# Sliding-window attention and soft MoE: the last experts' weights by column halves, with half-width stores ahead of the last load

## The chip, the core and the metric

The kernel runs on one core of a Trainium2 chip. The metric is the device time of one execution in microseconds. The engines are TensorE (PE; PEld its weight loads), VectorE (DVE), ScalarE (ACT), GpSimd (POOL) and SyncE (SP). Here POOL issues all loads, which turn fp32 in HBM into fp16 on the chip, and SP issues all stores.

## The reference

Eight batches of eight heads, 576 positions of 64 elements, go through causal attention with a window of 64. The result, 4608 rows of 512, goes through a soft mixture of eight experts with four slots each.

```python
scores = np.where((rel >= 0) & (rel < 64), q @ k.T / 8, -1e9)
x = (softmax(scores) @ v).transpose(0, 2, 1, 3).reshape(4608, 512)
logits = x @ phi                       # 4608 x 32 slots
slot_input = softmax(logits, axis=0).T @ x
for e in range(8):                     # 4 slots each
    h = np.maximum(slot_input[e] @ w1[e], 0.0)    # 512 -> 1024
    slot_out[e] = h @ w2[e]                       # 1024 -> 512
out = softmax(logits, axis=1) @ slot_out
```

Each slot's input is a sum over all 4608 rows, so no expert can start before the last row of attention is done, and no row of the result can be formed before the last expert is done.

## The kernel before

**Attention.** A unit is one batch and four of its heads; the sixteen units run one after the other, each in three stages j. `load_unit` issues three loads per unit from POOL. TensorE transposes (`stage_t1`, `stage_t2`), scores (`stage_s`) and weights the values (`stage_av`), ScalarE takes the exponential, VectorE divides and writes the rows x into `xbp`. Once both halves of a batch are there, six steps are spread over the next six stages: `stage_xt` (three transposes of x), `stage_logit` (logits, their exponential ET and column sums esum), `stage_ex` (ET transposed, row sums, their reciprocals crcp) and `stage_slot` (ET times x, added to acc). For the last batch, 7, no unit follows, and the six steps run one behind the other after the loop. Then acc is divided by the sum of esum and written as `slot_oa`, from which four small matmuls (`si`) make the slot inputs `slot_inT`.

**Weights.** `load_w(e, n)` loads a quarter of an expert: n = 0, 1 are halves of w1, n = 2, 3 halves of w2, 512 KB each as landed. They are issued between the units' loads, in the order of `w_order`, expert after expert; what is left at unit 13 is issued at once. A DMA of POOL waits for the eighth before it. w2 of expert 7 (tile `w2l`) has no buffer of its own: it takes one of the two of `xbp` (tag x_bp), after a batch pair is done with it.

**Experts.** `expert_h(e)` multiplies the slot inputs by w1 (16 matmuls of 256 columns, four at a time in different column groups), takes the ReLU on ScalarE, transposes h (`th`) and writes it as `hT`; `expert_o(e)` multiplies by w2 (8 matmuls of 512 columns) and adds into one PSUM tile `sop`. `expert_h(e + 1)` stands ahead of `expert_o(e)`. After expert 7, sop is cast to `slot_oa`, half by ScalarE and half by VectorE.

**The result.** For each of 9 blocks (8 batches, and one of the last 64 rows of all), four matmuls `cp` of 512 columns, each scaled by crcp on ScalarE or VectorE into `ob`, and two stores of 512 KB from SP. The buffers of ob are those of w1 (tag w1s).

**Order.** POOL issues as the code is written. On the other engines a scheduler sets the order, by dependencies and the order of the code.

Of the kernel before, what the change touches and what calls it, by code (L numbers as in the profile page):

```python
# [11 lines left out]
ALU = mybir.AluOpType  # L12
# [4 lines left out]
def kernel(  # L17
# [51 lines left out]
    w1_t, w2_t = {}, {}  # L69

    def load_w(e, n):
# [7 lines left out]
        if n < 2:  # L79
            c = slice(2 * n, 2 * n + 2)  # L80
            nc.gpsimd.dma_start(out=w1_t[e][:, c], in_=moe_w1[e].rearrange("(c p) f -> p c f", p=128)[:, c])  # L81
        else:
            c = slice(4 * n - 8, 4 * n - 4)
            nc.gpsimd.dma_start(out=w2_t[e][:, c], in_=moe_w2[e].rearrange("(c p) d -> p c d", p=128)[:, c])  # L84
# [43 lines left out]
    esum = const.tile([128, B + B // 2], FP32, name="esum")  # L128
# [137 lines left out]

    def stage_logit(b):
# [42 lines left out]

    nu = len(units)
    w_order = [(e, n) for e in range(E) for n in range(4)]
# [33 lines left out]
    stage_av(*pend)  # L346
    while todo:
        todo.pop(0)()
    b = B - 1
    stage_xt(b, 0)  # L350
    stage_xt(b, 1)
    stage_xt(b, 2)
    stage_logit(b)
    stage_ex(b)
    stage_slot(b)
    dinv = const.tile([128, 2], FP32, name="dinv")
    nc.vector.reduce_sum(dinv[:, 0:1], esum[:, :], axis=AXX)
    nc.vector.reciprocal(dinv[:, 1:2], dinv[:, 0:1])
    pa_sb = slot_oa
    nc.scalar.activation(pa_sb[:, 0:256], acc[:, 0:256], AF.Copy, scale=dinv[:, 1:2])  # L360
    nc.vector.tensor_scalar(out=pa_sb[:, 256:512], in0=acc[:, 256:512], scalar1=dinv[:, 1:2], scalar2=None, op0=ALU.mult)
# [4 lines left out]
    for dc in range(NHD):  # L366
        nc.tensor.matmul(si[:, dc, :], pa_sb[:, 128 * dc:128 * dc + 128], sel4[:, :], start=True, stop=True)
# [3 lines left out]
    sop = ps2.tile([128, D], FP32, name="sop", tag="sop", bufs=1)  # L371

    def expert_h(e):
# [6 lines left out]
        h_sb = pet.tile([128, 256], FP16, name="h_sb", tag="h_sb")  # L380
        nc.scalar.activation(h_sb[:, :], hp[:, :], AF.Relu)
        th = ps2.tile([128, 2, 4, SPE], FP32, name="th", tag="th", bufs=1)
        for f in range(2):
            nc.tensor.matmul(th[:, f], h_sb[:, 128 * f:128 * f + 128],
                             sel[:, :, SPE * e:SPE * e + SPE], start=True, stop=True)
# [6 lines left out]
    def expert_o(e):  # L392
        hT = hTs[e % 2]
        for i in range(NFC // 4):
            for g in range(4):
                nc.tensor.matmul(sop[32 * g:32 * g + 32, :], hT[:, 4 * i + g, :], w2_t[e][:, 4 * i + g, :],
                                 start=(e == 0 and i == 0), stop=(e == E - 1 and i == NFC // 4 - 1))

    expert_h(0)
    for e in range(E):  # L400
        if e + 1 < E:
            expert_h(e + 1)
        expert_o(e)
    nc.scalar.copy(out=slot_oa[:, 0:256], in_=sop[:, 0:256])
    nc.vector.tensor_copy(out=slot_oa[:, 256:512], in_=sop[:, 256:512])

    for blk in range(B + 1):
        ob = pw1.tile([128, 4, D], FP32, name="ob", tag="w1s")
        for g in range(4):
            cp = ps2.tile([128, D], FP32, name="cp", tag="cp", bufs=4)  # L410
            nc.tensor.matmul(cp[:, :], ET[:, 4 * blk + g, :], slot_oa[:, :],  # L411
                             start=True, stop=True)
# [5 lines left out]
        if blk < B:  # L418
            for g in range(0, 4, 2):
                nc.sync.dma_start(  # L420
                    out=out[S * blk + 128 * g:S * blk + 128 * g + 256, :].rearrange("(c p) d -> p c d", p=128),
                    in_=ob[:, g:g + 2, :])
        else:
            for o in range(2):
                nc.sync.dma_start(
                    out=out.rearrange("(c o t) d -> o t c d", o=2, t=S)[o, 512:576],
                    in_=ob[64 * o:64 * o + 64, :, :])

# [29 lines left out]
```

## Time and profile before

| | |
|---|---|
| median of 4 runs | 190.06 us (189.43 to 190.56) |
| the profiled execution: time, span | 189.43 us, 187.7 us |
| PE, DVE, ACT, POOL busy | 76%, 58%, 60%, 32% of the span |
| loads: landed by the POOL queue | 30.97 MB |
| stores: by the SP queue | 9.44 MB |
| granted TensorE clock, mean | 0.935 |

The span is from the first to the last instruction; the rest of the time lies around it. The bytes of loads are counted as they land, in fp16, so that 208 GB/s of loads are 416 GB/s read from HBM, while stores are fp32 on both sides. The DMA share is the mean busy share of the 16 DMA engines, and goes over 1 where transfers of one engine overlap. Rows of the profile carry line numbers of the kernel before.

### The profile page before, as it was taken

The page shows a single profiled execution, that of the slowest core. Times are in us where ns is not written, and L with a number is a line of the kernel's source. Part 1 is how long each engine was busy: PE and PEld are TensorE (multiplying, and loading weights), DVE is VectorE, ACT ScalarE, POOL GpSimd, SP SyncE. Part 2 cuts the span into 40 slices and gives each one's busy share as a digit, 9 for nine tenths or more (in the row PEclk, how much of TensorE's full clock was granted, in tenths as well). Part 3 has the DMA queues.
Part 4 walks back from the last instruction along what each step waited for, and adds up shares of the span by engine and source line. Part 5 has one row for each costly group of instructions (what it writes and reads, how often), then busy time and mean ns, then how long its engine had stood idle before and what let it go on. Part 6 is the DMA issues. An engine that isn't in the chain of part 4 may idle for free.

```text
span 187.7 us, 6583 instructions
## 1 busy us (share of the span) xinstructions
PE 143.3 (76%) x2912; PEld 101.3 (54%) x2912; DVE 109.0 (58%) x259; ACT 112.3 (60%) x189; POOL 59.6 (32%) x89
## 2 busy tenths in 40 slices
PE   0698998999988899899979989998567874985000
PEld 0476767767656676676856777676423541221000
DVE  2128678487666757866765984787842111997000
ACT  2557967968677496867869669684222221896000
POOL 7944444434343324434434342433310000000000
PEclk9999999999999999999999999999985999699555
DMA  4999999999999999999999999999999992699995
GB/s 61 173 201 207 207 210 205 206 210 207 209 206 207 211 206 208 207 207 209 207 208 206 207 207 208 208 210 211 207 209 207 210 186 38 263 406 404 409 386 147
DMA packets 31308, 40.83 MB, mean 218 GB/s; under 512 B 2096, under 2 KB 22576, under 8 KB 31280
## 3 DMA queue, kind: packets, MB, share of 16 engines
q0 software_dynamic: 26384, 30.97, 96.4%
q1 hardware_dynamic: 4896, 9.44, 13.5%
q8 instruction: 23, 0.38, 0.7%
q14 instruction: 5, 0.04, 0.1%
HBM read 61.93 MB, written 9.44 MB: 380 GB/s over the span
## 4 chain that ended last, share of the span: by engine, by line
PE 37%; ACT 26%; DMA 13%; DVE 7%; issue 7%; POOL 1%; DVEq 0%; ACTq 0%; POOLq 0%
ACT pm L199 12%; DMA w2l<-in_moe_w_dram 11%; PE tr L145 7%; PE tr L176 7%; ACT kT L152 6%; ACT qT L152 5%; PE sc L187 5%; PE sc L194 5%; DVE ob L417 4%; PE av L222 3%; DMA kn<-in_k_dram 3%; PE tr L259 3%; PE pa L304 2%; PE cp L411 2%; PE lt L270 2%
## 5 line engine op out<-in xcount | busy, mean ns | idle before, releaser
L199 ACT ACTIVATE pm<-sc 128x1024 f16<-128x1024 f32 (+1 forms) x48 | 39.6, 824 | 30.6 <-PE sc L194 30.3
L177 DVE COPY vw<-tr 128x1024 f16<-128x1024 f16 (+1 forms) x48 | 26.5, 553 | 7.3 <-PE tr L176 6.4
L176 PE MATMUL tr<-ident,vT 128*128 128x128 f16 x288 | 24.4, 222 | 1.7 <-DVE rc L228 1.6
L152 ACT COPY qT<-tr 128x640 f16<-128x640 f16 (+1 forms) x32 | 21.8, 744 | 4.4 <-PE tr L145 4.4
L152 ACT COPY kT<-tr 128x640 f16<-128x640 f16 (+1 forms) x32 | 22.0, 752 | 1.0 <-PE tr L145 1.0
L230 DVE TENSOR_TENSOR x_bp<-av,rc 128x512 f16<-128x512 f32 x32 | 22.0, 686 | 0.6
L187 PE MATMUL sc<-rep,hide 64*128 64x512 f16 (+1 forms) x96 | 20.4, 337 | 2.4 <-ACT pm L199 1.5
L176 PEld LDWEIGHTS <-vT 128*128 128x128 f16 x288 | 17.7, 99 | 5.9 <-issue 3.1
L222 PE MATMUL av<-vw,pm 128*64 128x65 f16 x576 | 18.9, 196 | 2.1 <-DVE x_bp L230 1.1
L194 PE MATMUL sc<-qT,kT 64*128 64x64 f16 x576 | 19.7, 192 | 0.2 <-issue 0.2
L222 PEld LDWEIGHTS <-pm 128*64 128x64 f16 x576 | 15.1, 111 | 7.2 <-issue 6.6
L194 PEld LDWEIGHTS <-kT 64*128 64x128 f16 x576 | 15.3, 95 | 4.7 <-issue 1.1
L145 PE MATMUL tr<-ident,qn 128*64 128x128 f16 x288 | 12.4, 232 | 6.7 <-DMA qn<-in_q_dram 5.4
L62 POOL DMA_DIRECT2D vn<-in_v_dram x16 | 11.5, 717 | 17.1 <-PE tr L176 5.8
L81 POOL DMA_DIRECT2D w1s<-in_moe_w_dram x16 | 11.3, 708 | 16.5 <-DMA w1s<-in_moe_w_dram 8.3
L84 POOL DMA_DIRECT2D w2s<-in_moe_w_dram x14 | 10.6, 754 | 18.9 <-DMA w1s<-in_moe_w_dram 11.8
L62 POOL DMA_DIRECT2D qn<-in_q_dram x16 | 11.5, 719 | 13.9 <-PE tr L145 5.1
L150 DVE COPY vT<-tr 128x512 f16<-128x512 f16 x16 | 11.6, 726 | 7.1 <-PE tr L145 7.1
L145 PE MATMUL tr<-ident,vn 128*64 128x128 f16 x288 | 12.7, 227 | 2.6 <-ACT kT L152 1.1
L145 PE MATMUL tr<-ident,kn 128*64 128x128 f16 x288 | 12.2, 228 | 2.8 <-issue 1.3
L228 DVE RECIPROCAL rc<-av 128x8 f32<-128x8 f32 x32 | 6.3, 197 | 13.7 <-PE av L222 13.7
L62 POOL DMA_DIRECT2D kn<-in_k_dram x16 | 11.5, 717 | 8.5 <-PE sc L194 2.5
(72 smaller groups left out, 216.7 us busy)
## 6 DMA issues: line engine op xcount, KB each, us to landing
out_dram<-ob SPq DMA_DIRECT2D x18, 512.0 KB, 6.4
w1s<-in_moe_w_dram POOLq DMA_DIRECT2D x16, 512.0 KB, 15.5
w2s<-in_moe_w_dram POOLq DMA_DIRECT2D x14, 512.0 KB, 13.4
qn<-in_q_dram POOLq DMA_DIRECT2D x16, 288.0 KB, 13.1
kn<-in_k_dram POOLq DMA_DIRECT2D x16, 288.0 KB, 13.5
vn<-in_v_dram POOLq DMA_DIRECT2D x16, 288.0 KB, 13.1
w2l<-in_moe_w_dram POOLq DMA_DIRECT2D x2, 512.0 KB, 19.7
phi_sb<-in_moe_phi_dram POOLq DMA_DIRECT2D x1, 32.0 KB, 7.2
```

Of the source, the lines that this page charges most:

```text
L62: nc.gpsimd.dma_start(out=t, in_=src[b, 4 * half:4 * half + 4].rearrange("(x h) (g t) d -> (h g) x (t d)", x=2, h=2, t=T))
L81: nc.gpsimd.dma_start(out=w1_t[e][:, c], in_=moe_w1[e].rearrange("(c p) f -> p c f", p=128)[:, c])
L145: nc.tensor.transpose(tr[64 * x:64 * x + 64, j, :], src[:, x, 64 * (t0 + j):64 * (t0 + j) + 64], ident[:, :])
L150: nc.vector.tensor_copy(out=o, in_=i)
L152: nc.scalar.copy(out=o, in_=i)
L176: nc.tensor.transpose(tr[:, 2 * w + h, :], st["vT"][:, h, 64 * i:64 * i + 128], ident[:, :])
L177: nc.vector.tensor_copy(out=st["vw"][:, wins[0]:wins[0] + n, :, 0:64], in_=tr[:, 0:2 * n, :].rearrange("p (w h) (x d) -> p w (h x) d", h=2 ...
L187: nc.tensor.matmul(sc[:, x, 0:128 * n], hide[64 * x:64 * x + 64, :], rep[64 * x:64 * x + 64, 0:2 * n, :], start=True, stop=False, skip_gro ...
L194: nc.tensor.matmul(sc[:, x, o:o + 64], st["kT"][64 * x:64 * x + 64, h, 64 * i:64 * i + 128], st["qT"][64 * x:64 * x + 64, h, 64 * i:64 * i ...
L199: nc.scalar.activation(pm[:, :, 0:2 * n, :], sc[:, :, 0:128 * n].rearrange("p x (w q) -> p x w q", q=64), AF.Exp, scale=scale)
L222: nc.tensor.matmul(av[r0:r0 + 64, kk, 65 * (w // 2):65 * (w // 2) + 65], pm[:, x, h * n + w, :], st["vw"][:, i, 2 * h + x, 0:65], start=Tr ...
L230: nc.vector.tensor_tensor(out=xb[:, c0:c0 + 2, 256 * half:256 * half + 256].rearrange("p c (k d) -> p k c d", d=64), in0=avv[:, :, :, 0:64 ...
```

## The change

Six things change.

1. *Rows in larger pieces.* w1 and, for experts 0 to 5, w2 give each partition neighbouring rows of HBM (in pairs, two transfers of them for w2; four for w1), so that the contiguous piece is twice as long. The matmuls' operands are picked with a stride to fit (`dc::NHD`, `f::2`).
2. *Column halves.* w2 of experts 6 and 7 is loaded in halves of 256 columns. Their w1 goes first, then the left halves of both, then the right halves.
3. *The last batch in parts.* Logits, transposes and slot sums of batch 7 are done for chunks 0-1, 2-3 and 4, interleaved in an order fixed by hand for PE, ACT and DVE; 13 dummy matmuls (`keep_busy`, 512 columns each) stand between them. The division by the total is folded in: acc is scaled while the last sums are on their way, and one instruction scales and adds the last part.
4. *Experts in an order fixed by hand*: `expert_h(e + 2)`, `expert_t(e + 1)` (the transposes of h, formerly the end of `expert_h`), then `expert_o(e)` in two halves of 256 columns, each into its own PSUM tile.
5. *Left halves first.* With the left halves of w2 of 6 and 7, the left half of the slots' outputs is cast, and blocks 0 to 3 are combined and stored in their left 256 columns. Only then come the right halves of 6 and 7, the right columns of blocks 0 to 3, and blocks 4 to 8 in full width.
6. *Casts*: the left half of slot_oa by ScalarE, the right half, later, by VectorE.

```diff
-            nc.gpsimd.dma_start(out=w1_t[e][:, c], in_=moe_w1[e].rearrange("(c p) f -> p c f", p=128)[:, c])
+            nc.gpsimd.dma_start(out=w1_t[e][:, c], in_=moe_w1[e].rearrange("(p c) f -> p c f", p=128)[:, c])
+        elif e >= E - NLAST:
+            c = slice(D // 2 * (n - 2), D // 2 * (n - 1))
+            nc.gpsimd.dma_start(out=w2_t[e][:, :, c], in_=moe_w2[e].rearrange("(c p) d -> p c d", p=128)[:, :, c])
         else:
-            c = slice(4 * n - 8, 4 * n - 4)
-            nc.gpsimd.dma_start(out=w2_t[e][:, c], in_=moe_w2[e].rearrange("(c p) d -> p c d", p=128)[:, c])
+            g = slice(2 * n - 4, 2 * n - 2)
+            nc.gpsimd.dma_start(out=w2_t[e].rearrange("p (g c) d -> p g (c d)", c=2)[:, g],
+                                in_=moe_w2[e].rearrange("(g p c) d -> p g (c d)", p=128, c=2)[:, g])
...
-    w_order = [(e, n) for e in range(E) for n in range(4)]
+    w_order = [(e, n) for e in range(E - NLAST) for n in range(4)]
+    last = range(E - NLAST, E)
+    w_order += [(e, n) for e in last for n in range(2)] + [(e, n) for n in range(2, 4) for e in last]
...
+    def keep_busy(n):
...
+        for _ in range(n):
+            nc.tensor.matmul(pd["kb"][:, 0, :], ident[:, :], rep[:, :, :].rearrange("p a b -> p (a b)"), start=True, stop=True)
...
+    def tail_sums():
+        nc.vector.reduce_sum(dinv[:, 0:1], esum[:, :], axis=AXX)
+        nc.vector.reciprocal(dinv[:, 1:2], dinv[:, 0:1])
+        nc.vector.tensor_scalar(out=acc[:, :], in0=acc[:, :], scalar1=dinv[:, 1:2], scalar2=None, op0=ALU.mult)
+        nc.vector.scalar_tensor_tensor(out=pa_sb[:, :], in0=moe["pa"][:, :], scalar=dinv[:, 1:2], in1=acc[:, :],
+                                       op0=ALU.mult, op1=ALU.add)
+        for part in range(3):
+            part_rs(B - 1, part)
...
+    with tc.manual_schedule(engines={mybir.EngineType.PE, mybir.EngineType.Activation, mybir.EngineType.DVE}):
+        stage_xt(b, 0)
+        stage_av(*pend)
+        part_lt(b, 0)
+        stage_xt(b, 1)
+        keep_busy(2)
+        part_te(b, 0)
+        stage_xt(b, 2)
+        part_pa(b, 0)
+        keep_busy(2)
+        part_lt(b, 1)
+        part_lt(b, 2)
+        keep_busy(3)
+        part_te(b, 1)
+        part_te(b, 2)
+        keep_busy(2)
+        part_pa(b, 1)
+        part_pa(b, 2)
+        keep_busy(4)
+        tail_sums()
...
+    NSPLIT = 4
+    whole = slice(0, D)
+    with tc.manual_schedule(engines={mybir.EngineType.PE, mybir.EngineType.Activation, mybir.EngineType.DVE}):
+        expert_h(0)
+        expert_h(1)
+        expert_t(0)
+        for e in range(E - NLAST):
+            expert_h(e + 2)
+            expert_t(e + 1)
+            expert_o(e, 0)
+            expert_o(e, 1)
+        expert_t(E - 1)
+        for e in last:
+            expert_o(e, 0)
+        slots_out(0)
+        for blk in range(NSPLIT):
+            combine(blk, halves[0])
+        for e in last:
+            expert_o(e, 1)
+        slots_out(1)
+        for blk in range(NSPLIT):
+            combine(blk, halves[1])
+        for blk in range(NSPLIT, B + 1):
+            combine(blk, whole)
```

The functions `part_lt`, `part_te`, `part_pa` and `part_rs` do for two chunks (or one) what `stage_logit`, `stage_ex` and `stage_slot` do for a batch; `combine` is the loop body of the blocks with a choice of columns, and `slots_out` the casts.

Where the order moves. On POOL, the last loads (w2l is expert 7's w2, w2s that of the others; sizes are partitions, then what each receives; rows that stand twice in a row are merged), before:

```order
L81 DMA w1s<-in_moe_w_dram 128x2x1024 x2
L84 DMA w2s<-in_moe_w_dram 128x4x512 x2
L81 DMA w1s<-in_moe_w_dram 128x2x1024 x2
L84 DMA w2l<-in_moe_w_dram 128x4x512 x2
L453 UNCONDITIONAL_BRANCH
```

and now:

```order
L82 DMA w1s<-in_moe_w_dram 128x2048 x4
L85 DMA w2s<-in_moe_w_dram 128x8x256
L85 DMA w2l<-in_moe_w_dram 128x8x256
L85 DMA w2s<-in_moe_w_dram 128x8x256
L85 DMA w2l<-in_moe_w_dram 128x8x256
L554 UNCONDITIONAL_BRANCH
```

Expert 7's w1 moved ahead of expert 6's w2, and a load of w2l now stands in the third place from the end as well as the last.

On VectorE, from the last exponential's sum to the slot inputs, before:

```order
L357 TENSOR_REDUCE dinv<-esum 128x1
L358 RECIPROCAL dinv<-dinv 128x1
L294 TENSOR_REDUCE rs<-te 128x5
L295 RECIPROCAL crcp<-rs 128x5
L309 TENSOR_TENSOR acc<-pa,acc 128x512
L361 TENSOR_SCALAR slot_oa<-acc,dinv 128x256
L368 CAST slot_inT<-si 128x128
```

and now:

```order
L367 TENSOR_REDUCE dinv<-esum 128x1
L368 RECIPROCAL dinv<-dinv 128x1
L369 TENSOR_SCALAR acc<-acc,dinv 128x512
L370 SCALAR_TENSOR_TENSOR slot_oa<-pa,dinv,acc 128x512
L316 TENSOR_REDUCE rs<-ex_3712 128x2
L317 RECIPROCAL crcp<-rs 128x2
L316 TENSOR_REDUCE rs<-ex_3744 128x2
L439 CAST slot_inT<-si 128x128
```

The row sums moved behind the instruction that writes slot_oa, and three of these short ones stand ahead of the cast of the slot inputs.

On VectorE, from the experts' last transposes to the end, before:

```order
L388 MEMSET hT_145 128x8x2
L389 CAST hT_145<-th 128x2x4x4
L388 MEMSET hT_147 128x8x2
L389 CAST hT_147<-th 128x2x4x4
L405 CAST slot_oa<-sop 128x256
L417 TENSOR_SCALAR ob<-cp,crcp 128x512 x18
```

and now:

```order
L463 MEMSET hT_147 128x8x2
L464 CAST hT_147<-th 128x2x4x4
L493 TENSOR_SCALAR ob<-cp,crcp 128x256 x8
L481 CAST slot_oa<-sop 128x256
L493 TENSOR_SCALAR ob<-cp,crcp 128x256 x8
L493 TENSOR_SCALAR ob<-cp,crcp 128x512 x10
```

Eight scalings of left halves moved ahead of the cast of the right half, which is the first instruction there that needs the right halves of w2. On SP, sixteen stores of half width (256 KB) stand where the first eight of 512 KB stood; ten whole ones follow, as before.

More of the change, by code (lines that the diff above doesn't have):

```diff
@@ L366 @@
     for dc in range(NHD):
-        nc.tensor.matmul(si[:, dc, :], pa_sb[:, 128 * dc:128 * dc + 128], sel4[:, :], start=True, stop=True)
+        nc.tensor.matmul(si[:, dc, :], pa_sb[:, dc::NHD], sel4[:, :], start=True, stop=True)
     nc.vector.tensor_copy(out=slot_inT, in_=si)
     sel = ident[:, :].rearrange("p (g s) -> p g s", s=NSLOT)
-    sop = ps2.tile([128, D], FP32, name="sop", tag="sop", bufs=1)
+    sop = [ps2.tile([128, D // 2], FP32, name="sop", tag="sop") for _ in range(2)]
+    h_t = {}
     def expert_h(e):
```

100 lines of the change are left out of this document (63 added, 37 removed).

## The prediction

> **What bounds the kernel now.** I read the profile's rate of the DMA engines first, in stretches that I chose after seeing where the page's GB/s line breaks (columns: stretch, its length, busy us and instruction count of PE, PEld, DVE, ACT and POOL, granted PE clock, DMA share, GB/s as they land: a load lands as fp16, two bytes for every four read).
>
> ```profile
> 20.00:100.00 80.00, 71.96 (x1675) 55.40 (x1673) 55.94 (x126) 60.29 (x101) 32.56 (x46) 1.00 1.20 208
> 138.50:141.50 3.00, 1.48 (x10) 0.39 (x10) 1.87 (x6) 0.86 (x4) 0.00 (x0) 0.63 1.18 208
> 143.50:146.50 3.00, 3.00 (x47) 1.51 (x41) 0.46 (x3) 0.77 (x2) 0.00 (x0) 0.57 1.19 210
> 152.00:153.00 1.00, 1.00 (x25) 0.59 (x24) 0.26 (x2) 0.11 (x1) 0.00 (x0) 1.00 1.23 212
> 153.00:154.00 1.00, 0.67 (x19) 0.64 (x23) 0.25 (x2) 0.27 (x1) 0.00 (x0) 1.00 1.07 172
> 154.00:155.00 1.00, 0.67 (x20) 0.26 (x12) 0.02 (x1) 0.38 (x1) 0.00 (x0) 1.00 0.73 120
> 155.00:156.00 1.00, 0.73 (x9) 0.19 (x8) 0.19 (x1) 0.00 (x0) 0.00 (x0) 1.00 0.58 97
> 156.00:157.40 1.40, 0.01 (x3) 0.01 (x2) 0.00 (x0) 0.00 (x0) 0.00 (x0) 1.00 0.28 45
> 157.40:160.20 2.80, 1.74 (x9) 0.68 (x9) 1.27 (x3) 1.44 (x3) 0.00 (x0) 0.92 0.00 0
> 160.20:161.20 1.00, 1.00 (x4) 0.38 (x3) 0.83 (x2) 0.89 (x2) 0.00 (x0) 0.50 0.04 14
> 161.20:182.00 20.80, 9.25 (x30) 2.77 (x28) 10.96 (x16) 9.70 (x15) 0.00 (x0) 0.75 1.05 406
> 182.00:186.00 4.00, 0.00 (x0) 0.00 (x0) 0.00 (x0) 0.00 (x0) 0.00 (x0) 0.50 0.85 247
> ```
>
> Up to 153 us the transfers run at 208 to 212 GB/s whatever the other engines do, and from 161.2 us the results leave at 406: the kernel is 150 us of loading and 25 us of storing, both at the rate of the DMA engines. Between them is a hole. Counting each stretch by what it lacks of 208 GB/s, the hole is 0.17 + 0.42 + 0.53 + 1.40 x 0.78 + 2.80 + 1.00 x 0.97 = 6.0 us of lost transfer. Its first part (153 to 157.4) is a ragged end, some DMA engines done four microseconds before others; its second (157.4 to 161.2) is a full stop. The chain of waits says what is in the stop.
>
> ```profile
> 137.54 19.80 DMA w2l<-in_moe_w_dram
> 157.35 0.04 issue
> 157.39 0.42 PE sop L396 x4
> 157.82 0.02 issue
> 157.84 0.38 ACT slot_oa L404
> 158.22 0.02 issue
> 158.24 0.43 DVE slot_oa L405
> 158.68 0.04 issue
> 158.72 0.39 PE cp L411
> 159.11 0.02 issue
> 159.13 0.70 ACT ob L415
> ```
>
> The last half of expert 7's second weight (tile w2l) lands at 157.35; four matmuls, two casts one after the other, one combine matmul and one scaling follow. The store queue starts right behind them:
>
> ```profile
> 160.19 0.43 SPq L420 DMA_DIRECT2D out_dram<-ob  x1
> ...
> L420 SPq DMA_DIRECT2D out_dram<-ob x16: 372/1070/1639, 160.2 to 177.1; - x16
> ```
>
> From 157.35 to the first stored bytes at 161.2 is 3.85 us. One execution is read here: its span is 187.7 us, its time 189.43, so 1.7 lie around the span; the median of the four runs, 190.06, is 0.6 above it. Savings are worked out in the span and taken off the median.
>
> **The change, part by part.** First the order of the last loads. Issue to landing, for all issues after 120 us, and the last issues:
>
> ```profile
> w1s<-in_moe_w_dram POOLq DMA_DIRECT2D x4, 512.0 KB, 19.8
> w2l<-in_moe_w_dram POOLq DMA_DIRECT2D x2, 512.0 KB, 19.7
> ...
> 132.45 0.71 POOL L81 DMA_DIRECT2D w1s<-in_moe_w_dram  x1 [1.80 <-DMA w1s<-in_moe_w_dram]
> 135.26 0.76 POOL L84 DMA_DIRECT2D w2l<-in_moe_w_dram  x1 [2.10 <-DVE x_bp L230]
> 137.54 0.74 POOL L84 DMA_DIRECT2D w2l<-in_moe_w_dram  x1 [1.52 <-DMA w2s<-in_moe_w_dram]
> ```
>
> A landing comes 19.8 us after its issue at a pitch of 2.5 us, so the last four positions land near 149.8, 152.3, 154.9 and 157.35. Now these four are column halves: left of expert 6, left of 7, right of 6, right of 7. The left halves of both are there at 152.3, five microseconds before the end. The w2l issue, which waits for VectorE at 135.26, moves one position forward, and right of 6 and right of 7 are queued on POOL behind it. If it still issues at 135.26 it is 2.8 us late for its position, but seven transfers (7 x 2.5 = 17 us) stand ahead in the DMA rings: cost nothing. Were that cover gone, the cost would be those 2.8 us.
>
> Size of the pieces: in w1 the contiguous piece doubles, in w2 of experts 0 to 5 it doubles, in the last four transfers it halves (256 columns). The stretches above with 208, 208 and 210 GB/s hold mostly q/k/v, w1 and w2 pieces, of different size (1152, 2048 and 1024 bytes landed); the rate moves by 1%. So I take 0 for both effects. Ends: 1% of the weights' 16.8 MB (81 us at 208) is 0.8 us gained; and if a half-size piece took a whole piece's time, the last 2.1 MB would need 20 us and not 10, so 10 us lost. No row shows a 512-byte piece; the 1% is much the nearest.
>
> The tail of attention (batch 7's slots) is cut into three parts with 13 dummy matmuls between them, in an order fixed by hand. Its end before:
>
> ```profile
> 139.37 1.03 PE L304 MATMUL pa<-x_bp,ex 128*32 128x512 f16 x5 [0.38 <-ACT ex L292]
> 140.44 0.69 DVE L309 TENSOR_TENSOR acc<-pa,acc 128x512 f32<-128x512 f32 x1 [0.54 <-PE pa L304]
> 141.17 0.51 ACT L360 ACTIVATE slot_oa<-acc,dinv 128x256 f16<-128x256 f32 x1 [1.85 <-DVE acc L309]
> 142.06 0.29 DVE L368 CAST slot_inT<-si 128x128 f16<-128x128 f32 x1 [0.54 <-PE si L367]
> 140.00:142.40 2.40, 0.69 (x5) 0.18 (x4) 1.33 (x3) 0.51 (x1) 0.00 (x0) 0.50 1.19 204
> ```
>
> The new last step (scale and add in one) is a 0.69 that takes the place of 0.69 + 0.51: 0.5 us sooner. The clock, 0.50 here, may stay at 1.00: the five matmuls' 1.03 would halve, 0.5 more. Against that stand the 13 dummies of 512 columns. Four such matmuls in different column groups took 0.42 in the chain above, five took 1.03 at half clock, two rounds of 0.5: a dummy, which fills all groups, costs 0.25 to 0.5 us, 3.3 to 6.5 in all, most of it while PE would wait. I take the slot inputs as ready at 142.3 as before, within 1.5 us either way. That is not on the path by itself; it moves the experts.
>
> ```profile
> 148.34 0.38 ACT L381 ACTIVATE h_sb<-hp 128x256 f16<-128x256 f32 x1 [1.13 <-PE hp L377]
> 149.85 0.38 ACT L381 ACTIVATE h_sb<-hp 128x256 f16<-128x256 f32 x1 [1.14 <-PE hp L377]
> ...
> 142.40:155.30 12.90, 10.94 (x200) 0.86 1.13 197
> ```
>
> Eight experts take 12.9 us, 1.51 each, and PE is busy 10.94 of them (PE's own view of that stretch: busy, clock, DMA). The old order must finish at 155.0, which was early enough for a landing at 157.35 and is too late for one at 152.3. The new order computes the first layer two experts ahead, so PE no longer waits for the ReLU in each round: at PE's 10.94, less the second layers of 6 and 7 that come later (4 x 0.4, from the four matmuls of 0.42), the chain ends near 151.8. The halved second layer doubles its weight loads (64 to 128), for which I add 0.5: 152.3, level with the landing. Had nothing come of it, it would be 155.0; kept as a rival.
>
> From left of 7 on: the path of the chain above without the second cast (0.43 + 0.02) and with a scaling of 256 columns for 512 (0.38 for 0.70, by the 256-column cast in the same chain) is 3.85 - 0.45 - 0.32 = 3.1 us. First stored bytes at 152.3 + 3.1 = 155.4, for 161.2. Four blocks of 512 rows by 256 columns are 2.1 MB, 5.2 us at 406 GB/s. Their scalings take 8 x 0.43 = 3.5 us on VectorE (the 0.43 cast above), under the 5.2. The eight stores issue in 0.37 to 0.43 us each when their ring is empty, under the 0.65 that each of 256 KB needs.
>
> Sharing with the loads: the last engines have loads until about 157.1, so 1.7 us of them at 155.4. Shared evenly with the stores, these take 3.4 us: right of 7 lands at 159.0. Its own 3.1 us follow: right-half bytes at 162.1. The engine that is last has 155.4 + 1.7 + 5.2 = 162.3 of work until then: it doesn't pause, with 0.2 to spare. From there on nothing differs: it stored from 161.2 to 186.0, 24.8 us with the slower end (247 GB/s, the 64-row transfers of the last block, which stay), and now does from 155.4 + 1.7 on. End 181.9 for 186.0. The sum: **4.1 us off the span**, 187.7 to 183.6; that execution 189.43 to 185.3; the median 190.06 to **186.0**.
>
> The 6.0 us of the hole aren't all to be had, since each store is spread over all engines and the ragged end makes the last engine the measure. If the raggedness goes too, the saving is 6.0 less what is lost before 155.4 (0.17 + 0.42 + 0.4 x 0.53 = 0.8): 5.2, with 0.8 of load pieces 6.0, so 184.1; the lower end is 0.9 below that, since the four runs alone lie 1.1 apart.
>
> Store pieces of 1 KB for 2 KB: 4.2 MB leaves in halves. No row shows them. Nearest, again, is that loads of 1 and 2 KB run alike: 0. The other end is the same time a piece, 203 GB/s: 4.2 MB in 20.7 for 10.3 us, 10.3 lost. The Trainium skill's DMA: Bandwidth & Descriptors (section Bandwidth) speaks against small transfers: it fits 2.0 us plus bytes over 436 GB/s to each, and asks for 1 MiB or more. By that, one at a time, sixteen of 256 KB are an estimated 41.6 us against 25.6 for eight of 512 KB, and the sum would be 202. This trace doesn't bear it out for a stream: 512 KB each would make 164 GB/s, and the row shows 406, several being in flight.
>
> **The rivals.** B, the loads starve: stores, once issued, go ahead of the last loads on every engine. For it: the store ring takes several transfers at once. Against it: nothing in the trace, where stores and loads never meet. Then right of 7 lands only after the left halves, at 162.3 + 0.3, its bytes come at 165.7, and 3.4 of the 4.1 us are given back as a new hole: 189.4. At half of that, 187.7. The skill's same page (Queues, rings and completion order) has each engine take turns between its rings, packet by packet; by that the even share holds and the sum is 186.0.
>
> C, the half pieces are slow on the store side; this is the one that ends slower. At the full price 186.0 + 10.3 = 196.3. It turns into a loss where the 4.2 MB take 4.1 us longer than 10.3, that is below 291 GB/s. Against it: 208 to 210 with every piece size. D, the same on the load side, at most 196; against it the same row.
>
> E, the change doesn't do what it says: the expert chain isn't shortened, or the dummies make it late. At 155.0 the first bytes come at 158.2, the last engine idles from 157.1, and 3.0 us are saved: 187.1. It would take 5.8 us of lateness to save nothing.
>
> **How the numbers follow.** Forecast 0.58 (183.4 to 187.6); B 0.16 (187.5 to 189.5, mostly still faster); E 0.08 (186.5 to 188.5); C 0.11, 0.08 of it slower; D 0.07, slower. A difference under 0.5% (0.95 us) can't be told from none. Faster: 0.58 + 0.13 + 0.08 = 0.79; same: 0.03 of B and 0.03 of C, 0.06; slower 0.15. Range: below 183.2 I leave 0.07, above 189.2 0.13 (C, D and little else).
>
> **What the profile after would show.** Right: first store bytes at 154.5 to 156.5; loads landing at 158 to 160; no stretch from 156 on under 300 GB/s store-equivalent (a load counted double) before the last 4 us; the 256-column stores at over 380 GB/s once alone. Wrong by B: landing of the last w2l beyond 161.5 and a hole behind the left halves. Wrong by C: a low rate with the DMA share at 1. By D: left of 7 landing well past 152.3 with the share still at 1.2. By E: the left halves' matmuls waiting for hT, not for a DMA. Most of all the forecast would be wrong if the last loads or the half stores ran at half rate.

## The result, and the profile after

The changed kernel takes 184.25 us (median of 11 runs, 183.71 to 185.86) against 190.19 for the kernel before on the same chips (16 runs): a ratio of 0.9702 [0.9679, 0.9725], 5.9 us less. Forecast were 186.0, within 183.2 to 189.2. The profiled execution of the changed kernel has a time of 183.95 and a span of 182.2; before, 189.43 and 187.7. The two traces differ by 5.5 us of span, and the account below is made in these.

The rate in the same kind of stretches (columns as in the prediction: busy us and count of PE, PEld, DVE, ACT and POOL, granted PE clock, DMA share, GB/s; a load counts once, as it lands):

```profile
20.00:100.00 80.00, 72.02 (x1685) 55.66 (x1684) 56.31 (x126) 60.38 (x102) 31.49 (x46) 1.00 1.16 209
138.50:141.50 3.00, 2.70 (x19) 1.05 (x17) 2.19 (x9) 0.83 (x6) 0.00 (x0) 1.00 1.06 214
...
151.00:153.00 2.00, 0.75 (x12) 0.52 (x12) 0.00 (x0) 0.41 (x2) 0.00 (x0) 1.00 1.45 197
153.00:154.00 1.00, 0.77 (x7) 0.36 (x5) 0.93 (x3) 1.00 (x3) 0.00 (x0) 1.00 0.98 139
154.00:155.00 1.00, 0.86 (x5) 0.44 (x4) 0.79 (x2) 1.00 (x3) 0.00 (x0) 0.74 0.97 170
155.00:156.00 1.00, 0.91 (x6) 0.36 (x4) 0.91 (x2) 0.79 (x3) 0.00 (x0) 0.50 1.27 299
156.00:157.00 1.00, 1.00 (x11) 0.43 (x10) 0.80 (x3) 0.72 (x2) 0.00 (x0) 0.50 1.16 345
157.00:158.00 1.00, 0.78 (x12) 0.24 (x8) 0.36 (x2) 0.00 (x0) 0.00 (x0) 0.50 1.10 386
...
160.00:161.00 1.00, 0.93 (x5) 0.36 (x3) 0.79 (x2) 0.98 (x3) 0.00 (x0) 0.50 0.94 330
...
180.00:180.50 0.50, 0.00 (x0) 0.00 (x0) 0.00 (x0) 0.00 (x0) 0.00 (x0) 0.50 0.32 119
180.50:181.00 0.50, 0.00 (x0) 0.00 (x0) 0.00 (x0) 0.00 (x0) 0.00 (x0) 0.50 0.00 0
```

The full stop is gone: between 153 and 180 no whole microsecond of these rows falls under 139 GB/s. Before, 157.4 to 160.2 had nothing at all. The last byte leaves near 180.5; before, near 186.0. In quarters of a microsecond from 150 to 160:

```profile
GB/s 195 199 199 195 197 197 197 197 197 201 199 190 229 127 102 98 98 94 207 283 291 297 309 299 309 320 371 381 385 389 393 377 365 393 377 393 389 389 381 365
```

From 153.25 the loads drop to half, some 98 GB/s: read by their rate, about half of the DMA engines have no load left. At 154.5 the stores set in. The trace doesn't name the engines, so that the stores run mainly on the idle ones is a reading of the rates.

The chain of waits around that point:

```profile
131.84 19.89 DMA w2l<-in_moe_w_dram
...
151.78 0.43 PE sop L473 x8
152.23 0.38 ACT slot_oa L479
...
152.65 0.28 PE cp L488
152.96 0.26 ACT ob L491
```

It has the steps of before, on 256 columns and with one cast, behind the left half of expert 7's w2, which lands at 151.74. Store queue, and the two w2l loads by their tile (durations of the issue, first and last start, then issue to landing):

```profile
153.64 18.96 SPq L496 DMA_DIRECT2D out_dram<-ob  x24
```

```profile
L85 POOL DMA_DIRECT2D w2l<-in_moe_w_dram x2: 873/877/881, 131.8 to 136.7; - x2
...
DMA to landing us min/median/max: 19.9/20.2/20.5
```

The first store is issued at 153.64 for 160.19. The right half, issued at 136.7, lands 20.5 us later, at 157.1, though stores run beside it.

The times between landing and last byte make up the account. Before, 28.65 us lay between the last landing (157.35) and the last byte (186.0): 3.85 without bytes and 24.8 of stores. Now 23.4 lie between 157.1 and 180.5. So 0.25 lies ahead of the last landing, 3.85 is the stop, and the time from there on is 1.4 shorter: 5.5. The bytes say where the 1.4 comes from. Both queues of the changed kernel from 154.5 to 157.1 (q1 holds the stores, q0 the loads; packets, MB, share of the 16 engines), then its stores from 157.1 to 180.6:

```profile
q1 hardware_dynamic: 643, 0.63, 68.9%
q0 software_dynamic: 355, 0.18, 51.0%
...
q1 hardware_dynamic: 6429, 8.81, 103.2%
```

0.63 MB had been stored before the last load landed. The other 8.81 MB took 23.4 us, a mean of 376 GB/s; before, 9.44 MB took 24.8, a mean of 381. The stores didn't become faster, less of them was left. The 0.25 is within the scatter of single traces: the last load lands at 157.35 in the trace of the kernel before and at 158.63 in that of b_tail2q, which has the same loads in the same order.

### The profile page after: what moved, and what is told of

Read it like the earlier page. It is cut to its first block, busy times and chain, and to the rows that moved or that the text cites. A ratio compares the mean times of both kernels' runs of the same rounds, so it can differ in the third digit from the quotient of the medians.

```text
span 182.2 us, 6834 instructions
## 1 busy us (share of the span) xinstructions
PE 145.6 (80%) x3009; PEld 104.6 (57%) x3009; DVE 111.5 (61%) x271; ACT 114.4 (63%) x200; POOL 57.1 (31%) x89
## 3 DMA queue, kind: packets, MB, share of 16 engines
q1 hardware_dynamic: 7072, 9.44, 14.3%
HBM read 61.93 MB, written 9.44 MB: 392 GB/s over the span
## 4 chain that ended last, share of the span: by engine, by line
PE 36%; ACT 27%; DMA 17%; issue 7%; DVE 4%; POOL 2%; ACTq 0%; POOLq 0%; DVEq 0%
ACT pm L204 11%; DMA w2l<-in_moe_w_dram 11%; ACT kT L157 7%; PE tr L181 7%; PE tr L150 6%; ACT qT L157 5%; PE sc L192 4%; PE sc L199 4%; DMA phi_sb<-in_moe_phi_dram 4%; PE cp L488 4%; PE av L227 3%; PE pa L356 2%; ACT ob L491 2%; PE tr L264 2%; DMA out_dram<-ob 2%
## 5 line engine op out<-in xcount | busy, mean ns | idle before, releaser
L493 DVE TENSOR_SCALAR ob<-cp,crcp 128x256 f32<-128x256 f32 (+1 forms) x26 | 14.6, 585 | 4.6 <-PE cp L488 4.3
L488 PE MATMUL cp<-slot_oa,ET 128*128 128x256 f16 (+1 forms) x52 | 14.3, 388 | 2.6 <-ACT ob L491 1.2
L491 ACT ACTIVATE ob<-cp,crcp 128x256 f32<-128x256 f32 (+1 forms) x26 | 13.7, 554 | 4.0 <-PE cp L488 3.5
```

Source lines behind the costliest of these rows:

```text
L491: nc.scalar.activation(ob[:, g, :], cp[:, :], AF.Copy, scale=cr)
```

## The experiments

The theory on trial: nearly all of the saving is store work brought ahead of and beside the last loads, and the rest of the change (pieces, tail, experts, dummies) only serves to have the left halves ready in time. The rivals give one of those parts, or the clock, a saving of its own. Each kernel is one edit of the changed kernel or of the one before. Times are medians, ratios are to the kernel before.

**a_whole: the changed kernel without early stores.** Both halves of w2 first, then all blocks in full width.

```diff
-        slots_out(0)
-        for blk in range(NSPLIT):
-            combine(blk, halves[0])
         for e in last:
             expert_o(e, 1)
+        slots_out(0)
         slots_out(1)
-        for blk in range(NSPLIT):
-            combine(blk, halves[1])
-        for blk in range(NSPLIT, B + 1):
+        for blk in range(B + 1):
             combine(blk, whole)
```

> The changed kernel with one part undone: after the experts all nine blocks are combined and stored at full width; the load order, the pieces, the last batch's parts and the experts' order stay. Theory 1 (the saving of 5.9 us is the stores that run beside the last loads and in the stop behind them): the right halves land near 157.1 us as before, the first stored bytes come 3.4 us later, near 160.5, and the 9.44 MB take 24.8 us again: 189.3 us, 0.8 to 1.0 below the kernel before. Theory 2 (larger pieces and the hand-set orders carry much of it): 187 us or less.

189.58 us, 0.9975 [0.9955, 0.9996]. Its chain of waits has the last load (start, us):

```profile
136.94 20.11 DMA w2l<-in_moe_w_dram
```

and SP's queue the first store:

```profile
160.16 18.00 SPq L496 DMA_DIRECT2D out_dram<-ob  x16
```

The load lands at 136.94 + 20.11 = 157.06. With everything else of the change in place, 5.3 of the 5.9 us are gone. The stop is back: 3.1 us from landing to the first issue. The theory holds. The run also serves as the reference for the meeting of loads and stores: without stores the last load lands at 157.06, with them at 157.1, and from 154.5 to 157.1 its loads are

```profile
q0 software_dynamic: 330, 0.16, 48.9%
```

0.16 MB, where 0.18 MB landed beside the stores. In this short meeting no cost to the loads is seen.

**b_pieces: the kernel before with the larger pieces alone.** w1 and w2 as rows in pairs and fours, all experts whole.

```diff
-            nc.gpsimd.dma_start(out=w1_t[e][:, c], in_=moe_w1[e].rearrange("(c p) f -> p c f", p=128)[:, c])
...
+            nc.gpsimd.dma_start(out=w1_t[e][:, c], in_=moe_w1[e].rearrange("(p c) f -> p c f", p=128)[:, c])
...
+                                in_=moe_w2[e].rearrange("(g p c) d -> p g (c d)", p=128, c=2)[:, g])
...
-        nc.tensor.matmul(si[:, dc, :], pa_sb[:, 128 * dc:128 * dc + 128], sel4[:, :], start=True, stop=True)
+        nc.tensor.matmul(si[:, dc, :], pa_sb[:, dc::NHD], sel4[:, :], start=True, stop=True)
...
-            nc.tensor.matmul(th[:, f], h_sb[:, 128 * f:128 * f + 128],
+            nc.tensor.matmul(th[:, f], h_sb[:, f::2],
```

> The kernel before with the first part of the change alone: w1 and all of w2 in pieces twice as long. Theory 1: the rate while weights land rises by 1 to 2%, the last load lands 0.3 to 0.8 us sooner than 157.35, and all of it reaches the end: 189.4 to 189.9 us for 190.2. Theory 2: the pieces are worth a larger share, 2 us or more: 188 us.

189.67 us, 0.9974 [0.9943, 1.0005]; the last load's row in its chain, which lands at 157.06:

```profile
137.63 19.44 DMA w2l<-in_moe_w_dram
```

The landing is 0.3 us earlier, which is within the scatter of single traces, and the time 0.5 less with an interval that reaches no change: the larger pieces may bring a few tenths, not more.

**a_nodummy: the changed kernel without the 13 dummies.**

```diff
-        keep_busy(2)
...
-        keep_busy(4)
```

> The changed kernel without the 13 dummy matmuls. Theory 1 (they are off the path): the granted clock falls to 0.50 for some 3 us after 140 us, the experts' chain loses what slack it has (the first left-half matmul of expert 7 waited 0.98 us for its load), and the time is 184.2 to 184.8 us. Rival: the lower clock makes the chain 2 to 3 us late, the first stores leave at 156 us or later, and the time is 185.5 to 186.5 us.

184.57 us, 0.9708 [0.9677, 0.9740]: by the medians not to be told from the changed kernel. Yet the clock differs as intended. Its stretches, and those of the changed kernel:

```profile
140.00:142.00 2.00, 1.15 (x7) 0.38 (x7) 1.67 (x6) 0.18 (x1) 0.00 (x0) 0.50 1.05 209
142.00:150.00 8.00, 7.62 (x171) 5.18 (x174) 1.82 (x13) 2.30 (x6) 0.00 (x0) 0.69 1.34 200
```

```profile
140.00:142.00 2.00, 1.62 (x27) 0.90 (x28) 1.73 (x8) 0.00 (x0) 0.00 (x0) 1.00 1.06 213
142.00:150.00 8.00, 7.69 (x226) 5.69 (x222) 1.69 (x12) 2.94 (x8) 0.00 (x0) 1.00 1.34 199
```

The clock is 0.50 and 0.69 without the dummies and 1.00 with them. (Of the seven traces with all dummies, six have 1.00 from 136 to 142 us; that of a_as128 has 0.59 from 136 to 140.) The first store then goes out at

```profile
155.08 18.93 SPq L491 DMA_DIRECT2D out_dram<-ob  x24
```

1.4 us later than with them. The profiled execution of this run took 185.07, 1.1 more than the 183.95 of the changed kernel's. It is one of the two slowest of its six (183.83 to 185.38), and the medians lie only 0.3 apart. So whether the work that the dummies speed up has slack stays open: the medians see no loss, the two traces do.

**a_oldexperts: the first layer one expert ahead, as before.**

```diff
-        expert_h(1)
         expert_t(0)
-        for e in range(E - NLAST):
-            expert_h(e + 2)
+        for e in range(E - 1):
+            expert_h(e + 1)
             expert_t(e + 1)
-            expert_o(e, 0)
-            expert_o(e, 1)
-        expert_t(E - 1)
+            if e < E - NLAST:
+                expert_o(e, 0)
+                expert_o(e, 1)
```

> The changed kernel with the experts in the order before: first layer one expert ahead, its transposes right behind it; the rest stays. By the prediction's step the eight experts take some 12.9 us again from 141.6 us, ready near 154.5 and not at 150.5, first stored bytes near 157.5 and not 154.6. Theory 1 (the DMA engines that end their loads last, near 156.6, set the end): only what comes after 156.6 counts, 0.8 to 1.3 us lost: 185.0 to 185.6 us. Rival (each microsecond of the first store counts): 187 us. Second rival (nothing there is on the path): 184.3 us.

187.08 us, 0.9868 [0.9821, 0.9914]: 2.8 us lost. That is the rival's figure (each microsecond of the first store counts, 187); the theory that only what comes after 156.6 counts asked for 185.0 to 185.6, and it fails here. The profiled execution, 189.23, is some 2 us above the other three; its clock was low until some 151, so the period is read after that. The ReLU of each expert in that trace (in brackets: ScalarE's wait):

```profile
146.61 0.38 ACT L454 ACTIVATE h_sb<-hp 128x256 f16<-128x256 f32 x1 [2.22 <-PE hp L450]
149.21 0.38 ACT L454 ACTIVATE h_sb<-hp 128x256 f16<-128x256 f32 x1 [2.22 <-PE hp L450]
...
153.44 0.38 ACT L454 ACTIVATE h_sb<-hp 128x256 f16<-128x256 f32 x1 [1.36 <-PE hp L450]
155.19 0.38 ACT L454 ACTIVATE h_sb<-hp 128x256 f16<-128x256 f32 x1 [1.36 <-PE hp L450]
```

and in the changed kernel:

```profile
144.70 0.38 ACT L454 ACTIVATE h_sb<-hp 128x256 f16<-128x256 f32 x1 [0.75 <-PE hp L450]
145.83 0.38 ACT L454 ACTIVATE h_sb<-hp 128x256 f16<-128x256 f32 x1 [0.74 <-PE hp L450]
```

One expert takes 1.13 us with two ahead, and with one ahead 1.75 at full clock (2.60 at the low one). That is more than the 1.51 of the kernel before. A reading that fits the rows: PE's order, fixed by hand, has the transposes and what follows them wait for the ReLU. The two-ahead order is needed: it is the part of the change, next to the early stores, that carries the most.

**a_oldtail: the last batch's steps as before, one behind the other.**

```diff
+    stage_av(*pend)
+    while todo:
+        todo.pop(0)()
     b = B - 1
-    with tc.manual_schedule(engines={mybir.EngineType.PE, mybir.EngineType.Activation, mybir.EngineType.DVE}):
-        stage_xt(b, 0)
-        stage_av(*pend)
-        part_lt(b, 0)
...
-        keep_busy(4)
-        tail_sums()
+    stage_xt(b, 0)
+    stage_xt(b, 1)
+    stage_xt(b, 2)
+    stage_logit(b)
+    stage_ex(b)
+    stage_slot(b)
+    nc.vector.reduce_sum(dinv[:, 0:1], esum[:, 0:B + B // 2], axis=AXX)
...
```

> The changed kernel with the last batch as it was: logits, sums and division of batch 7 in one piece behind each other, in the scheduler's order, no dummies; the rest stays. The slot inputs come near 142.4 us for 141.5 and the clock falls to 0.50 there; the experts' chain is later by 1 to 2 us, the first stores by as much (154.6 to 156 or 157). Theory 1 (the engines with loads until 156.6 set the end): 0 to 0.8 us lost, 184.3 to 185.1 us. Rival (that the tail was a needed part): 186 us.

186.13 us, 0.9787 [0.9759, 0.9814]: 1.9 lost; the rival of the expectation (186) has it right, the theory (0 to 0.8 lost) has not. First store:

```profile
156.99 18.40 SPq L489 DMA_DIRECT2D out_dram<-ob  x24
```

3.35 us later than in the changed kernel. The tail's order and its dummies together are worth far more here than in the forecast, which had its end unchanged and off the path.

**a_split2: two blocks of left halves, not four.** `NSPLIT = 2`.

> The changed kernel with the left halves of two blocks ahead of the right halves of w2 in place of four (1.05 MB, 2.6 us of stores). Theory 1: the stores run out near 159.4 us on the engines that were last with their loads, the first right halves leave near 160, so 0.5 to 1.2 us of pause, less 0.3 for fewer half-width pieces: 184.5 to 185.2 us. Rival (two blocks are enough, or half-width pieces cost more than the pause): 184.2 us or less.

185.43 us, 0.9767 [0.9733, 0.9800]: 1.2 lost. In the stretches:

```profile
158.00:159.00 1.00, 1.00 (x5) 0.56 (x5) 0.47 (x2) 0.69 (x2) 0.00 (x0) 0.50 0.47 164
159.00:160.00 1.00, 1.00 (x5) 0.43 (x4) 0.96 (x4) 0.96 (x3) 0.00 (x0) 0.50 0.07 24
```

The stores run out before results of the right halves are there: between 158 and 160, 1.5 of two microseconds are missing (at some 390 GB/s). Two blocks don't fill the time, four do.

**b_early: how loads and stores share.** The kernel before; 16 stores of 256 KB from a tile that is ready early, issued while loads run. The results of blocks 0 to 3 aren't computed.

```diff
+    early = pld.tile([128, D], FP32, name="early", tag="qn")
+    nc.vector.memset(early, 0.0)
+    nc.vector.tensor_copy(out=early[:, 0:NSLOT], in_=si[:, 0, :])
+    for blk in range(4):
+        for g in range(4):
+            nc.sync.dma_start(out=out[S * blk + 128 * g:S * blk + 128 * g + 128, :], in_=early)
...
-    for blk in range(B + 1):
+    for blk in range(4, B + 1):
```

> Measures what stores do to loads. The kernel before, with the results of blocks 0 to 3 left out: sixteen stores of 256 KB (2 KB pieces, 4.2 MB) leave instead from a tile without results, as soon as the slot inputs are there near 142.4 us, beside the last 15 us of loads; blocks 4 to 8 as before. Theory A (even share, the prediction's): the loads are held up by nearly what the stores take while both run: the last load lands at 160 us or later, by a fully even share near 167, and the end is at 184 us or later. Theory B (loads are not held up, as in the changed kernel, where the last load landed at 157.1 with stores beside it and at 157.1 without): it lands within 1 us of 157.35, the stores fill the room that loads leave, and the rest ends near 178 us, 180 us of time. Theory C (stores go first): it lands near 167.6.

188.52 us, 0.9941 [0.9913, 0.9970]. The last load, in the chain:

```profile
138.79 29.13 DMA w2l<-in_moe_w_dram
```

SP's queue with the early stores, and the stretches ahead of the first results:

```profile
143.48 18.81 SPq L374 DMA_DIRECT2D out_dram<-early  x16
```

```profile
168.00:170.00 2.00, 1.07 (x6) 0.39 (x6) 0.42 (x1) 0.37 (x1) 0.00 (x0) 0.50 0.17 67
170.00:172.50 2.50, 2.50 (x8) 0.82 (x7) 1.73 (x3) 2.03 (x3) 0.00 (x0) 0.50 0.08 30
```

The load lands at 138.79 + 29.13 = 167.92. From issue to landing it takes 29.13 us where it took 19.80 before: over a long meeting the loads are held up by 9.3 us. (The landing is 10.6 later than before, but the load was also issued 1.25 later, ahead of the first of these stores.) 4.2 MB of stores at 406 GB/s need 10.3. The landing alone doesn't tell an even share from stores that go first, which the expectation has at 167.6; the rates of the two queues from 153 to 160 do:

```profile
q0 software_dynamic: 664, 0.73, 59.9%
q1 hardware_dynamic: 671, 1.22, 52.7%
```

The loads move 0.73 MB in 7 us, 104 GB/s, half of their 208; the stores 174, somewhat under half of their 406. So they share about evenly. The Trainium skill says the same (DMA: Bandwidth & Descriptors, Queues, rings and completion order: each engine takes its rings in turn, packet by packet), and this trace agrees. The end was expected at 184 or later, and 188.52 is well beyond: the stop between the last load and the first result is back, at 168 to 172.5, because nothing was left to store in it. Stores only pay where they fill that stop.

**a_blk8first: the block of last rows ahead of blocks 4 to 7.** Its two stores have 64 partitions, and end the span at a lower rate in both kernels.

```diff
-        for blk in range(NSPLIT, B + 1):
+        for blk in [B] + list(range(NSPLIT, B)):
             combine(blk, whole)
```

> The changed kernel with the block of the last 64 rows combined and stored ahead of blocks 4 to 7 and not at the end. If the low store rate of the last four microseconds (323 to 339 GB/s in the changed kernel, 247 before) belongs to the 64-row transfers, they now share the engines with 128-row ones and the end comes 0.5 to 0.9 us sooner: 183.4 to 183.8 us. If it belongs to the engines running dry one after the other, it stays at the end whatever stands there: 184.2 us within 0.3.

185.90 us, 0.9788 [0.9758, 0.9817]: slower than the changed kernel by 1.65 where 0.5 to 0.9 less was expected. A miss. Its rows:

```profile
166.00:171.00 5.00, 2.34 (x8) 0.57 (x6) 3.60 (x6) 2.98 (x5) 0.00 (x0) 1.00 1.01 294
...
176.00:180.00 4.00, 0.00 (x0) 0.00 (x0) 0.00 (x0) 0.00 (x0) 0.00 (x0) 0.50 1.05 408
```

The end now runs at 408, but the low rate has moved with the 64-row stores to 166 to 171 us (294): whole stores beside them don't fill it. Five microseconds at 294 for 406 lose 1.4; the changed kernel loses 1.1 at its end from 176 on (338, 309 and 119 GB/s). That makes 0.3 of the 1.65. The trace is of the fastest of the seven runs (184.79), and the rest stays open.

**a_tail2q and b_tail2q: the two 64-row stores from two queues.** The second goes out from ScalarE's queue, in the changed kernel and in the one before.

```diff
-                nc.sync.dma_start(
+                (nc.sync, nc.scalar)[o].dma_start(
```

> The changed kernel with the very last store (64 rows, the second of the last block's two) issued by ScalarE's queue in place of SyncE's, so that the two 64-row transfers run side by side. Theory 1 (a 64-row transfer keeps only part of the DMA path busy, and two that write from different halves of the partitions fill each other's room): the last four microseconds, now at 323 to 339 GB/s, rise towards 400, 0.4 to 0.8 us off: 183.5 to 183.9 us. Rival (they are slow for another reason, their small count of rows or the engines running dry): 184.25 us within 0.3.

> The same in the kernel before, where the last four microseconds ran at 247 GB/s: theory 1, that the changed kernel's end was cheaper by about 1 us because its engines finish out of step, says that there is more to be had here, 1.0 to 1.6 us: 188.5 to 189.1 us for 190.1. Rival: no change, 190.1 within 0.4.

185.49 us, 0.9758 [0.9731, 0.9785], 1.2 more than the changed kernel; and 191.56, 1.0078 [1.0048, 1.0108], 1.4 more than the kernel before. The two weren't side by side, so the question stays open. In the second kernel ScalarE's store is out at 173.87 and SP's last one at 182.67:

```profile
173.87 0.72 ACTq L425 DMA_DIRECT2D out_dram<-ob  x1
```

```profile
182.67 1.18 SPq L425 DMA_DIRECT2D out_dram<-ob  x1
```

SP had waited 2.2 us for a store to land. While one 64-row store ran with nothing beside it, its stretch reads

```profile
178.50:180.50 2.00, 0.00 (x0) 0.00 (x0) 0.00 (x0) 0.00 (x0) 0.00 (x0) 0.50 0.97 215
```

One such store alone moves 215 GB/s, about half of 406. Whether two at once reach the whole was not settled by these. Much of the loss lies ahead of the stores. The profiled execution of the second kernel took 191.67, 2.2 more than that of the kernel before; its last load was issued 0.9 us later and lands at 158.63, 1.3 later, and the first store follows at 161.48 for 160.19:

```profile
138.45 20.18 DMA w2l<-in_moe_w_dram
```

Why the load is late is open.

**b_as128 and a_as128: the last block's stores with 128 partitions.** The rate of the end without its cause. They write into rows of block 0, so the last 64 rows of each batch are left out of the result.

```diff
-            for o in range(2):
-                nc.sync.dma_start(out=..., in_=ob[64 * o:64 * o + 64, :, :])
+            for g in range(0, 4, 2):
+                nc.sync.dma_start(out=out[128 * g:128 * g + 256, :].rearrange("(c p) d -> p c d", p=128),
+                                  in_=ob[:, g:g + 2, :])
```

> Measures what the form of the last block's stores costs. The kernel before; the last block's results (64 rows of each batch, as two stores of 64 partitions) go out as two stores of 128 partitions over rows of block 0 instead, so that the bytes, the pieces and the place in the queue stay and only the number of partitions changes (the last 64 rows of each batch are left out). Theory 1: 64 partitions feed only half of the path (where such a store ran alone it moved some 200 GB/s), so the last microseconds rise from 247 to 406 GB/s: 1.05 MB in 2.6 for 4.2 us, 1.6 us off: 188.5 us, 188.1 to 188.9. Rival: the engines run dry there whatever the form, 190.0 within 0.4.

> The same in the changed kernel. Theory 1 with the steps of the two groups of DMA engines out of time (those done with the loads early are ahead of the others, so that 64-row transfers of one group run beside 128-row ones of the other): only some 0.6 us is left to win, 183.6 us, 183.2 to 184.0, and the difference to what the kernel before wins (about 1 us) is the part of the change's saving that the prediction's sum lacked. Rival: the same 1.6 us as in the kernel before, 182.7 us, and the sum lacked something else.

190.12 us, 0.9999 [0.9980, 1.0018]; and 184.51, 0.9702 [0.9674, 0.9730]. Neither gains. The last stretches of the kernel before with this edit:

```profile
180.00:184.00 4.00, 0.00 (x0) 0.00 (x0) 0.00 (x0) 0.00 (x0) 0.00 (x0) 0.50 1.05 408
...
184.50:186.50 2.00, 0.00 (x0) 0.00 (x0) 0.00 (x0) 0.00 (x0) 0.00 (x0) 0.50 0.14 53
```

and of the changed kernel with it:

```profile
176.00:180.00 4.00, 0.00 (x0) 0.00 (x0) 0.00 (x0) 0.00 (x0) 0.00 (x0) 0.50 1.05 408
...
180.50:181.00 0.50, 0.00 (x0) 0.00 (x0) 0.00 (x0) 0.00 (x0) 0.00 (x0) 0.50 0.61 230
```

The rate was a hit: whole stores run at 408 up to 184, where 182 to 186 had 247. The time was a miss in both; the rival of b_as128 (190.0 whatever the form) has its time right. In the kernel before with this edit, the last 2 us move 53 GB/s at a DMA share of 0.14: two of sixteen engines' worth of work, still storing when the others are done. This remainder takes the place of the slow 64-row end. In the changed kernel with it, it isn't there; all end within half a microsecond. Its trace doesn't say that whole stores are worth nothing, though: its first store went out at 156.02, 2.4 us later than in the changed kernel's trace, behind a clock of 0.59 at 136 to 140 us and with the same order of instructions up to there, and its time, 184.41, is only 0.46 longer. A gain at the end and a loss from the late start may cancel there.

No version beat the changed kernel.

## Why the prediction was right, and where it was off

- **The mechanism holds.** The forecast gave the saving to the stop between last load and first store; a_whole shows it, 5.3 of 5.9 us. The sum was short: 4.1 us off the span were forecast, 5.5 were measured. The points below say where.
- **First landing and first bytes: right, each somewhat sooner than forecast.** Left of 7 forecast at 152.3, measured 151.74; first bytes forecast at 155.4, measured 154.5. The w2l issue came at 131.84, ahead of the 135.26 that the forecast allowed for.
- **Experts: right in kind, somewhat long.** The chain was to end at 151.8 to 152.3; its last ReLU was over by 150.1, and the left half of 7 waited for its load. It began 0.8 us earlier than before, and the 0.5 added for the doubled weight loads wasn't needed. The period of 1.13, eight times, is 9.0, for 10.94 - 1.6 = 9.3. a_oldexperts shows that one expert ahead would have missed the landing (first store 159.74 in its trace): rival E was a real one, had the order not been changed.
- **Sharing: wrong in this place, without effect.** Right of 7 was to land at 159.0, by an even share with the stores; it landed at 157.1. b_early has the even share where both run for long. Why it did not show in some 2.5 us (0.18 MB of loads landed from 154.5 on, 0.16 without stores) isn't settled; by the rate of 98 GB/s, about half of the engines had no loads left then. Rival B is refuted: the loads starve neither here nor in b_early.
- **The step that was off: the last engine as the measure.** The forecast let the engine whose loads end last begin its stores at 155.4 + 1.7 = 157.1, and gave it all of the 24.8 us from there: end 181.9. Measured is 180.5, 23.4 after 157.1. The sum put at nothing what is stored while some loads still run. Those 0.63 MB, 1.65 us at the mean of 381 GB/s, less 0.25 for the somewhat lower mean of 376 for the rest, are the 1.4. The forecast's other sum, 5.2 us if the raggedness goes too, comes nearest to the 5.5 of the spans, in part by luck: it starts from first bytes at 155.4, which came at 154.5.
- **What stays open there.** The trace doesn't tell the engines apart, so how bytes stored early shorten an end that is spread over all engines isn't shown. One reading is that the engine that is slowest with stores isn't the one that ends its loads last. b_as128 has a late remainder of few engines and a_as128 hasn't; but a_as128 began to store as the loads ended (0.05 MB before 157.1), so its early start can't be what removed it. The Trainium skill (DMA: Bandwidth & Descriptors, Latency and other measured facts) has two of the sixteen usually slower, and its guess at a cause is for transfers issued by GpSimd; these stores are SP's, and no run here shows which engines are late. Nor were the 24.8 us mainly such a remainder. The end of the kernel before:

```profile
182.00:185.00 3.00, 0.00 (x0) 0.00 (x0) 0.00 (x0) 0.00 (x0) 0.00 (x0) 0.50 0.98 281
185.00:186.00 1.00, 0.00 (x0) 0.00 (x0) 0.00 (x0) 0.00 (x0) 0.00 (x0) 0.50 0.44 143
```

  9.44 MB at 406 GB/s are 23.25, 1.5 less than 24.8. Of these, 0.9 lie in the first row, at a share of nearly 1 with the 64-row stores running, and 0.6 in the last microsecond, where few engines work.

- **Size of the pieces: forecast 0, measured small and of both signs.** Larger load pieces land at 209 for 208 over the attention and at 214 in 138.5 to 141.5 (b_pieces: 0.5 us gained, if anything). The column halves, with 512 bytes landed, run at 197. The 1 KB stores run at 386 for 406 (157 to 158 us), about 0.5 us on 4.2 MB. Rivals C and D asked for half rate; 5% was measured. The fit of the Trainium skill that the prediction set beside its sum (DMA: Bandwidth & Descriptors) is given there for transfers issued by GpSimd, each by itself; SP's 256 KB stores, several in flight, ran at 386 GB/s and don't follow it.
- **Tail and dummies: the cost was right, the worth was not.** Four dummies take 1.04 us, 0.26 each, the low end of the forecast, and the slot inputs were ready 0.8 earlier than before, within its 1.5. But the forecast called the tail no part of the path by itself: a_oldtail loses 1.9 us. What lateness costs is best read with each trace's first store beside the time of its own execution: 153.64 and 183.95 (changed kernel), 155.08 and 185.07 (a_nodummy), 156.99 and 186.44 (a_oldtail), 159.74 and 189.23 (a_oldexperts). A microsecond later costs 0.8, then 0.7, then 1.0. If the last engine were the measure, the first microseconds would be free; they aren't here. These are single executions, and by the medians the first step (0.3) isn't clear of noise.

Against the forecast's signs for the profile after: first bytes at 154.5, at the edge of its 154.5 to 156.5; the landing at 157.1, below its 158 to 160; the half-width stores at 386 alone, as it said; one dip to 330 at 160, none that matters.

## What to carry to other kernels

Where a kernel loads to its end and then stores, look at what lies between the last landing and the first store, and order the last loads so that enough finished results exist to fill exactly that gap: four blocks did, two didn't, and stores spread over the loads (b_early) only moved the gap. Don't count on slack in what prepares the first store: in the traces here each microsecond of its lateness cost 0.7 to 1.0, also while loads still ran. And when the gain is worked out, count the bytes that are stored ahead of the last landing as off the end, at the mean rate of the store phase; a sum that waits for the last engine left out 1.4 us here.

## What was not expected of the hardware

- A store from 64 partitions alone moves 215 GB/s where 128 partitions move 406, at a DMA share of 0.97 (b_tail2q). Put elsewhere it slows that place (294 over 5 us, a_blk8first).
- After the last common store a few engines' worth of work remains for 2 us in b_as128 (53 GB/s at a share of 0.14), and not in a_as128; what makes the difference is open.
- By their rate, the DMA engines don't end their loads together: from 153.25 to 154.5 half of it (98 for 197) remains, and the last load lands at 157.1.
- The same order of instructions gave a clock of 1.00 in one kernel's trace and 0.59 in another's at 136 to 140 us. Where PE waits for each ReLU, as in a_oldexperts, it fell to 0.50 (146 to 150 us) in spite of the dummies ahead.
